# Each pair of last-transform results in a buffer of its own, in a tile whose data are dead

## The chip, the cores and the metric

The kernel runs on one core of one Trainium2 chip. The metric is the device time of one execution, in microseconds (us). Time before: 134.21 us, the median of three runs (134.1 to 134.49).

## The reference

```python
def _A_ref(x, w_r, w_i):                                   # x: 1 x 2048 x 512
    X = jnp.fft.rfft2(x.astype(jnp.float32), axes=(-2, -1))
    X = X * (w_r + 1j * w_i)
    return jnp.fft.irfft2(X, s=(S, D), axes=(-2, -1)).astype(jnp.bfloat16)

def _B_ref(x, w1, b1, w2, b2):
    u = _gelu(jnp.einsum("bsd,sf->bdf", _layernorm(x), w1) + b1)   # S=2048 -> F=1792
    return (jnp.einsum("bdf,fs->bds", u, w2) + b2).transpose(0, 2, 1)

g = _sigmoid((x * gate_w).sum(-1, keepdims=True))
return g * _A_ref(x, w_r, w_i) + (1 - g) * _B_ref(x, w1, b1, w2, b2)
```

All inputs and the output are bfloat16. Branch A filters the 2048 x 512 input in the Fourier domain. Branch B is a layer norm and a two-layer MLP that mixes tokens. A gate g, one number per row, blends the two.

## The kernel before, in words

**Tiling.** The 2048 output rows are cut into 16 blocks of 128, numbered j. Branch B's second product needs, for each j, 14 matmuls of 128x128 by 128x512 (`m2`, L978 to L983) that add up in one PSUM bank. PSUM, the memory in which TensorE leaves its results, has eight banks here: four called `acc`, two `fa`, two `fb`. Block 15 is computed in three column parts (256, 128 and 128 columns), the last two in an `fa` and an `fb` bank.

**The last transform.** Branch A ends with a product with the table `tg` for each j (`i3`, L937 to L946): ten small matmuls for the two blocks of a pair (j, j + 1), five of them into an `fa` bank and five into an `fb` bank. There are eight pairs; I number them 0 to 7. Then:

- `i3ev` (L950 to L955) runs on ScalarE (ACT): it reads one bank, multiplies it by g and writes a half of the pair's tile `eo` ("eviction" below). This frees the bank.
- `es` (L958 to L969) runs on VectorE (DVE): one small copy and two additions or subtractions from `eo` into `es`, two more from `es` back into `eo`, in place. This unfolds a symmetry of the transform. For the last pair (j of at least `LATE` = 14) it first adds a bias (L963), and its results go straight into the output tile `tb_` (shown as `x` in the profile, whose place in memory it takes).
- `yev` (L987 to L990) on ACT moves block j of branch B out of its `acc` bank, with bias and 1 - g, into `tb_`, for j under 14; I call it y with the number of the block.
- `fin` (L992 to L995) on DVE adds a pair's `eo` to `tb_`. For blocks 14 and 15 `fin` is another operation (L998 to L1002), which adds a PSUM bank times 1 - g to `tb_`: one of 512 columns for block 14, then one of 256 and two of 128 for block 15.
- `store` (L1005 to L1009) is a DMA that SyncE (SP) issues: blocks 0-3, 4-7, 8-11, 12-13, 14, and the three parts of 15.

**Buffers.** `eo` has two buffers (`NEO` = 2), 2 KB per partition each. Pair k + 2 can be evicted only when pair k's `fin` has read its buffer. For the last pair, `es` itself is the last reader.

**Order.** Every piece of work is a task with an engine, an estimated duration, its dependencies, a priority, and the buffers that it takes (`alloc`) and gives back (`free`). `Plan.order` (L173 to L239) plays the tasks through an event simulation: whenever an engine is free it takes the ready task with the lowest priority number whose buffers are there. The resulting order is written out, and each engine executes its own list strictly in that order. `i3` has priority 4 and `m2` 20 + j, so a pair's transform goes ahead of the second product as soon as the plan sees an `fa` and an `fb` bank free. On ACT y has priority 1 and an eviction 1.5.

**The tile `B`.** `t["B"]` (L317), 16 KB per partition, holds the spectrum. Its last readers are the matmuls of the transform before this one (`i1`, L856 to L876). After them nobody uses it.

The functions that the diff touches:

Of the kernel before, what the change touches and what calls it, by code (L numbers as in the profile page):

```python
# [13 lines left out]
BF16 = mybir.dt.bfloat16  # L14
F32 = mybir.dt.float32

P = 128
S = 2048
D = 512
NJ = 16  # L20
F = 1792
NFT = 14
L = 256
# [116 lines left out]
class Plan:  # L140
# [11 lines left out]
    def add(self, eng, dur, emit, reads=(), writes=(), prio=0.0, alloc=(), free=(), nbytes=0, after=()):  # L152
        t = Task()
        t.eng, t.dur, t.emit, t.prio = eng, dur, emit, prio
        t.alloc, t.free, t.nbytes = tuple(alloc), tuple(free), nbytes
        t.users, t.end, t.ready = [], None, 0.0
        deps = set(after)
        for k in reads:
            if k in self.last_w:
                deps.add(self.last_w[k])  # L160
            self.readers.setdefault(k, []).append(t)
        for k in writes:
            if k in self.last_w:
                deps.add(self.last_w[k])
            deps.update(self.readers.get(k, ()))
            self.last_w[k] = t
            self.readers[k] = []
        deps.discard(t)
        t.deps = deps
        self.tasks.append(t)  # L170
        return t
# [70 lines left out]
def tt(n):  # L242
    return 0.07 + n / 1920.0
# [10 lines left out]
def act(n, ptr=0):  # L254
    return 0.065 + 0.09 * ptr + n / 1200.0
# [12 lines left out]
def kernel(  # L268
# [22 lines left out]

    pool = ctx.enter_context(tc.tile_pool(name="sb", bufs=1))
    psum = ctx.enter_context(tc.tile_pool(name="ps", bufs=1, space=bass.MemoryType.PSUM))
    NEO, NES = 2, 1

    def sb(shape, dt, tag, bufs=1):
        return pool.tile(shape, dt, tag=tag, name=tag, bufs=bufs)
# [2 lines left out]
        return psum.tile(shape, dt, tag=tag, name=tag, bufs=bufs)  # L300

    NB = {"acc": 4, "fa": 2, "fb": 2}
    caps = {"wa": 1, "wb": 2, "xf": 2, "eo": NEO, "es": NES, **NB}
    pl = Plan(caps)
    add = pl.add
    t = {}
# [156 lines left out]
    for r in range(4):  # L463
# [3 lines left out]
        for b, qs in enumerate(groups):  # L467
            js = [4 * q + r for q in qs]
            xb = [xk[q] for q in qs]
            g = (r, b)  # L470
# [38 lines left out]
            for j in js:  # L509
                if j in HACT:  # L510
                    add("ACT", 0.71, lambda j=j: A.activation(t["h"][:, j // 4, j % 4, :], t["x"][:, j // 4, j % 4, :], ActF.Identity,  # L511
                                                                  bias=t["nmr"][:, j:j + 1], scale=t["rstd"][:, j:j + 1]),
                        reads=xb + [("rstd", *g)] + mvk, writes=[("h", j)], prio=-0.5 + 0.1 * r)
# [19 lines left out]
        for dq in range(4):  # L533
            def fa(r=r, dq=dq):
# [8 lines left out]
                free=["xf"] if dq == 3 else ())  # L543
            add("ACT", act(512), lambda r=r, dq=dq: A.copy(t["X"][:, :, r, :, dq, :], t["pa", r, dq][:]),  # L544
                reads=[("pa", r, dq)], writes=[("X", r, dq)], prio=0, free=["fa"])
# [160 lines left out]
    gates = []  # L706
# [225 lines left out]
    for grp in groups:  # L932
        for j in grp:
            q, r = j // 4, j % 4
            tag = ("fa", "fb")[j % 2]

            def i3(j0=j):  # L937
                g = t["tg"]
                for j in (j0, j0 + 1):
                    p3 = t["i3", j] = ps([P, 2, L], F32, ("fa", "fb")[j % 2], 2)  # L940
                    zv = [xph(h).rearrange("p (q v r a) -> p q v r a", q=4, v=2, r=4)[:, j // 4, :, j % 4, :] for h in range(2)]
                    T.matmul(p3[:, 0, 0:129], lhsT=zv[0][:, 0], rhs=g[:, 0:129], start=True, stop=False)
                    T.matmul(p3[:, 0, 0:129], lhsT=zv[0][:, 1], rhs=g[:, 512:641], start=False, stop=True)
                    T.matmul(p3[:, 0, 129:256], lhsT=zv[0][:, 1], rhs=g[:, 129:256], start=True, stop=True)
                    T.matmul(p3[:, 1, 0:128], lhsT=zv[1][:, 0], rhs=g[:, 256:384], start=True, stop=True)
                    T.matmul(p3[:, 1, 128:256], lhsT=zv[1][:, 1], rhs=g[:, 384:512], start=True, stop=True)  # L946
            if j % 2 == 0:
                add("PE", mm(*[129] * 10), i3, reads=[("z", 0), ("z", 1), "tg"], writes=[("i3", j), ("i3", j + 1)], prio=4, alloc=["fa", "fb"])
                for i in (j, j + 1):
                    def i3ev(j=i):  # L950
                        if j % 2 == 0:
                            t["eo", j // 2] = sb([P, 2, 2, L], BF16, "eo", NEO)
                        A.activation(t["eo", j // 2][:, j % 2], t["i3", j][:], ActF.Copy, scale=t["g"][:, j:j + 1])  # L953
                    add("ACT", act(512, 1), i3ev, reads=[("i3", i), "g"] + ([("eo", j)] if i % 2 else []), writes=[("eo", i)], prio=1.5,
                        alloc=["eo"] if i % 2 == 0 else (), free=[("fa", "fb")[i % 2]])  # L955
                eok = [("eo", j), ("eo", j + 1)]

                def es(j=j + 1):  # L958
                    e, s = t["eo", j // 2], sb([P, 2, 2, 2, P], BF16, "es", NES)
                    o = e if j < LATE else (tbuf(j), t["tb_"][:, j - 1:j + 1])[1]  # L960
                    if j >= LATE:
                        for i in range(2):
                            V.tensor_scalar_add(e[:, i, 0, 0:129], e[:, i, 0, 0:129], t["ombb2"][:, j - 1 + i:j + i])  # L963
                    o = o[:].rearrange("p j h (k d) -> p j (h k) d", k=2)
                    V.tensor_copy(s[:, :, :, :, 0], e[:, :, :, 0:129:128].rearrange("p j h k -> p j k h"))  # L965
                    V.tensor_add(s[:, :, 0, :, 1:P], e[:, :, :, 1:P], e[:, :, :, P + 1:L])
                    V.tensor_sub(s[:, :, 1, :, P - 1:0:-1], e[:, :, :, 1:P], e[:, :, :, P + 1:L])  # L967
                    V.tensor_add(o[:, :, 0:4:3], s[:, :, :, 0], s[:, :, :, 1])  # L968
                    V.tensor_sub(o[:, :, 2:0:-1], s[:, :, :, 0], s[:, :, :, 1])  # L969
                late = j >= LATE  # L970
                add("DVE", tiny(1) + 4 * tt(512) + (0.3 if late else 0), es, reads=(eok + ["omg"]) if late else [],
                    writes=[("o", j), ("o", j + 1)] if late else eok, prio=4, alloc=["es"],
                    free=["eo", "es"] if late else ["es"], after=gates if late else ())

            parts = [slice(0, D)] if j < NJ - 1 else [slice(0, L), slice(L, L + P), slice(L + P, D)]
            for n, cs in enumerate(parts):
                for ft in range(NFT):
                    def m2(ft=ft, j=j, q=q, r=r, n=n, cs=cs):  # L978
                        if ft == 0:
                            t["y", j, n] = ps([P, D], F32, ("acc", "fa", "fb")[n], (4, 2, 2)[n])  # L980
                        w, o = w2at(ft)
                        T.matmul(t["y", j, n][:, cs], lhsT=w[:, o, 512 * q + r:512 * q + 512:4], rhs=t["gl"][:, ft, cs],  # L982
                                 start=(ft == 0), stop=(ft == NFT - 1))  # L983
                    add("PE", mm(cs.stop - cs.start), m2, reads=[("w2", ft), ("gl", ft)], writes=[("y", j, n)], prio=20 + j + 0.3 * n,
                        alloc=[("acc", "fa", "fb")[n]] if ft == 0 else (), after=m1t[-16:-15] if ft == 0 else ())
            if j < LATE:
                def yev(j=j):  # L987
                    A.activation(tbuf(j).rearrange("p h d -> p (h d)"), t["y", j, 0][:], ActF.Identity, bias=t["ombb2"][:, j:j + 1],  # L988
                                 scale=t["omg"][:, j:j + 1])
                add("ACT", act(512, 2), yev, reads=[("y", j, 0), "omg"], writes=[("o", j)], prio=1, free=["acc"], after=gates)  # L990
                if j % 2:
                    def fin(j=j):  # L992
                        o = t["tb_"][:, j - 1:j + 1]
                        V.tensor_add(o, o, t["eo", j // 2][:])  # L994
                    add("DVE", tt(1024), fin, reads=eok, writes=[("o", j - 1), ("o", j)], prio=4, free=["eo"])  # L995
            else:
                for n, cs in enumerate(parts):
                    def fin(j=j, n=n, cs=cs):  # L998
                        o = tbuf(j).rearrange("p h d -> p (h d)")[:, cs]
                        V.scalar_tensor_tensor(o, t["y", j, n][:, cs], t["omg"][:, j:j + 1], o, op0=Alu.mult, op1=Alu.add)  # L1000
                    add("DVE", d1(cs.stop - cs.start) + 0.1, fin, reads=[("y", j, n), "omg", ("o", j)], writes=[("of", j, n)], prio=1,
                        free=[("acc", "fa", "fb")[n]])  # L1002

        for n, cs in enumerate(parts):
            def store(grp=grp, cs=cs):  # L1005
                q, r0, r1 = grp[0] // 4, grp[0] % 4, grp[-1] % 4 + 1
                dma(o4[:, q, r0:r1, cs], t["tb_"][:, grp[0]:grp[-1] + 1].rearrange("p j h d -> p j (h d)")[:, :, cs])
            add("SP", 0.5, store, reads=[("o", j) for j in grp] + [("of", j, n) for j in grp if j >= LATE], prio=50,
                nbytes=256 * (cs.stop - cs.start) * len(grp))  # L1009
# [35 lines left out]
```

## Time and profile before

| | |
|---|---|
| median of the runs | 134.21 us |
| the profiled execution | 134.02 us |
| its span, first to last instruction | 132.2 us |
| PE busy | 124.5 us, 94% |
| DVE busy | 110.8 us, 84% |
| ACT busy | 83.5 us, 63% |
| granted TensorE clock, mean | 0.997 |

How to read it: PE is TensorE's matmuls and PEld its weight loads, DVE is VectorE, ACT is ScalarE, SPq the queue of SyncE, which issues DMAs. A row of the timeline gives its start and its length in us, then the engine, the line of the kernel, the operation, the tile written and the tile read, and how many instructions the row merges. A bracket at the end is the idle time of the engine before the row, and what ended it. Consecutive matmuls overlap, so a row's length is longer than the distance to the next start. Everything that the change touches lies in the last 28 us of the span.

### The profile page before, as it was taken

The page shows a single profiled execution, that of the slowest core. Times are in us where ns is not written, and L with a number is a line of the kernel's source. Part 1 is how long each engine was busy: PE and PEld are TensorE (multiplying, and loading weights), DVE is VectorE, ACT ScalarE, POOL GpSimd, SP SyncE. Part 2 cuts the span into 40 slices and gives each one's busy share as a digit, 9 for nine tenths or more (in the row PEclk, how much of TensorE's full clock was granted, in tenths as well). Part 3 has the DMA queues.
Part 4 walks back from the last instruction along what each step waited for, and adds up shares of the span by engine and source line. Part 5 has one row for each costly group of instructions (what it writes and reads, how often), then busy time and mean ns, then how long its engine had stood idle before and what let it go on. Part 6 is the DMA issues. An engine that isn't in the chain of part 4 may idle for free.

```text
span 132.2 us, 2156 instructions
## 1 busy us (share of the span) xinstructions
PE 124.5 (94%) x766; PEld 70.8 (54%) x780; DVE 110.8 (84%) x248; ACT 83.5 (63%) x166; POOL 0.2 (0%) x4
## 2 busy tenths in 40 slices
PE   6899999999999999999999999999899999999970
PEld 2345454545554575744445555455686665655660
DVE  2689999999999995089999999999859567979790
ACT  4568989599999999993220062322899366583700
POOL 0000000000000000000000000000000000000000
PEclk9999999999999999999999999999999999999998
DMA  3999999936599376999979200000000000330322
GB/s 91 377 359 392 395 394 380 370 79 132 89 272 273 76 159 228 294 397 409 423 299 358 112 0 0 7 0 2 0 0 0 5 0 16 142 159 5 159 79 79
DMA packets 17478, 23.18 MB, mean 175 GB/s; under 512 B 1574, under 2 KB 14908, under 8 KB 17468
## 3 DMA queue, kind: packets, MB, share of 16 engines
q1 hardware_dynamic: 17180, 22.59, 50.3%
q10 hardware_dynamic: 288, 0.46, 1.2%
q8 instruction: 6, 0.10, 0.3%
q14 instruction: 4, 0.03, 0.1%
HBM read 20.93 MB, written 2.10 MB: 174 GB/s over the span
## 4 chain that ended last, share of the span: by engine, by line
DVE 35%; DMA 30%; SPq 13%; PE 11%; issue 4%; ACT 3%; DVEq 0%; ACTq 0%
DMA wa<-in_B_w_dram 15%; SPq L309 13%; PE acc L982 6%; DMA wb<-in_B_w_dram 5%; DMA wt<-in_A_w_i_dram 5%; DMA W<-in_A_w_r_dram 3%; DVE xp L807 3%; DVE st L807 3%; ACT eo L953 3%; DVE xp L812 2%; DVE st L578 2%; DVE B L819 2%; DVE xp L813 2%; DVE eo L968 2%; DVE es L967 2%
## 5 line engine op out<-in xcount | busy, mean ns | idle before, releaser
L982 PE MATMUL acc<-gl,wb 128*128 128x512 bf16 (+1 forms) x108 | 27.2, 372 | 0.3
L982 PE MATMUL acc<-gl,wa 128*128 128x512 bf16 (+1 forms) x109 | 26.4, 372 | 0.1
L684 PE MATMUL acc<-h,wb 128*128 128x512 bf16 x108 | 24.9, 379 | 0.1
L988 ACT ACTIVATE x<-acc,ombb,omg 128x512 bf16<-128x512 f32 x14 | 10.7, 779 | 21.2 <-PE acc L982 21.2
L982 PEld LDWEIGHTS <-wb 128*128 128x128 bf16 x126 | 13.5, 114 | 9.7 <-issue 0.2
L982 PEld LDWEIGHTS <-wa 128*128 128x128 bf16 x126 | 13.5, 114 | 9.6
L684 PE MATMUL acc<-h,wa 128*128 128x512 bf16 x61 | 16.9, 379 | 1.1 <-DVE h L505 0.8
L684 PEld LDWEIGHTS <-wb 128*128 128x128 bf16 x112 | 10.9, 98 | 11.7
L684 PEld LDWEIGHTS <-wa 128*128 128x128 bf16 x112 | 10.3, 98 | 10.8 <-issue 1.9
L700 ACT ACTIVATE gl<-acc,b1f 128x512 bf16<-128x512 f32 x11 | 7.6, 695 | 6.8 <-PE acc L684 6.8
L478 DVE BATCH_NORM_STATS2 stats<-x 128x6 f32<-128x512 bf16 x14 | 9.4, 673 | 2.2 <-DMA x<-in_A_x_dram 2.2
L544 ACT CAST X<-fa 128x512 bf16<-128x512 f32 x16 | 9.3, 583 | 2.6 <-PE fa L541 2.4
L714 ACT ACTIVATE x<-x 128x512 bf16<-128x512 bf16 x16 | 10.1, 657 | 0.0
L511 ACT ACTIVATE h<-x,nmr,rstd 128x512 bf16<-128x512 bf16 x13 | 9.8, 806 | 0.4 <-DVE nmr L502 0.2
L684 PE MATMUL fb<-h,wa 128*128 128x512 bf16 x32 | 9.4, 379 | 0.0
L953 ACT ACTIVATE eo<-fa,g 128x512 bf16<-128x512 f32 x8 | 5.5, 688 | 3.5 <-DVE x L994 3.5
L965 DVE COPY es<-eo 128x8 bf16<-128x8 bf16 x8 | 1.5, 188 | 5.2 <-ACT eo L953 4.8
L684 PE MATMUL fa<-h,wa 128*128 128x512 bf16 x16 | 5.6, 379 | 0.0
L953 ACT ACTIVATE eo<-fb,g 128x512 bf16<-128x512 f32 x8 | 5.5, 691 | 0.0
L359 PE MATMUL fa<-xp 128*128 128x512 bf16 x10 | 4.3, 618 | 1.2 <-DVE xp L320 1.2
L653 ACT CAST B<-fb 128x512 bf16<-128x512 f32 x8 | 5.0, 627 | 0.0
L653 ACT CAST B<-fa 128x512 bf16<-128x512 f32 x8 | 4.9, 615 | 0.0
(177 smaller groups left out, 233.1 us busy)
## 6 DMA issues: line engine op xcount, KB each, us to landing
wb<-in_B_w_dram SPq DMA_DIRECT2D x11, 512.0 KB
wa<-in_B_w_dram SPq DMA_DIRECT2D x7, 512.0 KB
wa<-in_B_w_dram SPq DMA_DIRECT2D x3, 896.0 KB
x<-in_A_x_dram SPq DMA_DIRECT2D x3, 512.0 KB
wb<-in_B_w_dram SPq DMA_DIRECT2D x4, 384.0 KB
out_dram<-x SPq DMA_DIRECT2D x3, 512.0 KB
rot<-dft_ti SPq DMA_DIRECT2D x1, 736.5 KB
rot<-dft_ta SPq DMA_DIRECT2D x4, 160.0 KB
```

The lines of the kernel that those rows point to most:

```text
L309: (eng or nc.sync).dma_start(out=out_ap, in_=in_ap)
L478: V.bn_stats(out=t["stats"][:, j, :], in_=t["x"][:, j // 4, j % 4, :])
L511: add("ACT", 0.71, lambda j=j: A.activation(t["h"][:, j // 4, j % 4, :], t["x"][:, j // 4, j % 4, :], ActF.Identity, bias=t["nmr"][:, j:j ...
L544: add("ACT", act(512), lambda r=r, dq=dq: A.copy(t["X"][:, :, r, :, dq, :], t["pa", r, dq][:]), reads=[("pa", r, dq)], writes=[("X", r, dq ...
L653: A.copy(t["B"][:, lt, e, 2 * c:2 * c + 2, :].rearrange("p s (i b) -> p s i b", b=4), t["pb", lt, e, c][:].rearrange("p s b i -> p s i b"))
L684: T.matmul(t["u", ft][:], lhsT=w[:, j // 4, j % 4, c * P:(c + 1) * P], rhs=t["h"][:, j // 4, j % 4, :], start=(j == jorder[0]), stop=(j == ...
L700: gelus.append(add("ACT", act(512, 1) , lambda ft=ft: A.activation(t["gl"][:, ft, :], t["u", ft][:], ActF.Gelu_apprx_tanh, bias=t["b1f"][: ...
L714: A.activation(t["x"][:, q, r, :], t["x"][:, q, r, :], ActF.Copy, accum_out=t["glog"][:, 4 * q + r:4 * q + r + 1])
L807: V.tensor_mul(o, xs, w)
L953: A.activation(t["eo", j // 2][:, j % 2], t["i3", j][:], ActF.Copy, scale=t["g"][:, j:j + 1])
L982: T.matmul(t["y", j, n][:, cs], lhsT=w[:, o, 512 * q + r:512 * q + 512:4], rhs=t["gl"][:, ft, cs], start=(ft == 0), stop=(ft == NFT - 1))
L988: A.activation(tbuf(j).rearrange("p h d -> p (h d)"), t["y", j, 0][:], ActF.Identity, bias=t["ombb2"][:, j:j + 1], scale=t["omg"][:, j:j + 1])
```

## The change

The tile tag `eo` with its two buffers goes. At pair 0 one tile of eight pairs, 16 KB per partition, is allocated under the tag `B`, that is, in the place of the spectrum; each pair gets its own eighth. The tasks no longer take or give back `eo`, so nothing in the plan bounds how many evicted pairs may be under way except the `fa` and `fb` banks.

```diff
-    NEO, NES = 2, 1
+    NES = 1
...
-    caps = {"wa": 1, "wb": 2, "xf": 2, "eo": NEO, "es": NES, **NB}
+    caps = {"wa": 1, "wb": 2, "xf": 2, "es": NES, **NB}
...
                         if j % 2 == 0:
-                            t["eo", j // 2] = sb([P, 2, 2, L], BF16, "eo", NEO)
+                            if j == 0:
+                                t["eo"] = sb([P, NJ // 2, 2, 2, L], BF16, "B")
+                            t["eo", j // 2] = t["eo"][:, j // 2]
...
-                    add("ACT", act(512, 1), i3ev, ..., writes=[("eo", i)], prio=1.5,
-                        alloc=["eo"] if i % 2 == 0 else (), free=[("fa", "fb")[i % 2]])
+                    add("ACT", act(512, 1), i3ev, ..., writes=[("eo", i)], prio=1.5, free=[("fa", "fb")[i % 2]])
...
-                    free=["eo", "es"] if late else ["es"], after=gates if late else ())
+                    free=["es"], after=gates if late else ())
...
-                    add("DVE", tt(1024), fin, reads=eok, ..., prio=4, free=["eo"])
+                    add("DVE", tt(1024), fin, reads=eok, ..., prio=4)
```

No instruction is added or removed. Since the plan is made from these tasks, the engines' lists change, as they stand in the kernel as built:

- **ACT.** Before: y8, y9, four evictions, y10, four evictions, y11, four, y12, two, y13, two. After: y8, y9, ten evictions, y10, six evictions, y11, y12, y13. Of the waits before an eviction, those on DVE for a buffer are gone, except that the very first eviction waits for what DVE and one DMA did with the spectrum; all other evictions wait for PE alone, or for nothing.
- **PE.** The list is the same up to its entry 1276 and from 1425 on, of 1562. Between, pairs 4 to 7 come earlier among the second product's matmuls: pair 4 three matmuls after pair 3, then pair 5 after three more, pair 6 after three, pair 7 after six. Before, pair 4 came 17 matmuls after pair 3, and pair 7 followed the second matmul of block 13.
- **DVE.** The same list but for one step: the addition of pair 6 (`fin`) goes behind `es` of pair 7.
- **SP.** The same stores in the same order.

More of the change, by code (lines that the diff above doesn't have):

```diff
@@ L951, in i3ev @@
                         if j % 2 == 0:
-                            t["eo", j // 2] = sb([P, 2, 2, L], BF16, "eo", NEO)
+                            if j == 0:
+                                t["eo"] = sb([P, NJ // 2, 2, 2, L], BF16, "B")
+                            t["eo", j // 2] = t["eo"][:, j // 2]
                         A.activation(t["eo", j // 2][:, j % 2], t["i3", j][:], ActF.Copy, scale=t["g"][:, j:j + 1])
-                    add("ACT", act(512, 1), i3ev, reads=[("i3", i), "g"] + ([("eo", j)] if i % 2 else []), writes=[("eo", i)], prio=1.5,
-                        alloc=["eo"] if i % 2 == 0 else (), free=[("fa", "fb")[i % 2]])
+                    add("ACT", act(512, 1), i3ev, reads=[("i3", i), "g"] + ([("eo", j)] if i % 2 else []), writes=[("eo", i)], prio=1.5, free=[("fa", "fb")[i % 2]])
                 eok = [("eo", j), ("eo", j + 1)]
@@ L994, in fin @@
                         V.tensor_add(o, o, t["eo", j // 2][:])
-                    add("DVE", tt(1024), fin, reads=eok, writes=[("o", j - 1), ("o", j)], prio=4, free=["eo"])
+                    add("DVE", tt(1024), fin, reads=eok, writes=[("o", j - 1), ("o", j)], prio=4)
             else:
```

## Prediction

> **What bounds the kernel now.** I read the table of waits first, because the change takes a wait away, then the timeline of the last 28 us, where all of it happens. From the table of waits (who waited for whom: us in total, times, longest):
>
> ```profile
> ACT x L988 <- PE acc L982: 21.2, 8, 7.7
> ...
> DVE es L965 <- ACT eo L953: 4.8, 4, 2.4
> ACT eo L953 <- DVE x L994: 3.5, 2, 2.3
> ```
>
> The last two make a ring: the eviction waits for the buffer that `fin` (L994) gives back, and `es` waits for the eviction. ACT's wait for PE is harmless: there is work enough on PE. The timeline shows one turn of the ring:
>
> ```profile
> 120.88 1.28 DVE L994 TENSOR_TENSOR x<-x,eo 128x1024 bf16<-128x1024 bf16 x2
> ...
> 121.66 0.69 ACT L953 ACTIVATE eo<-fa,g 128x512 bf16<-128x512 f32 x1 [2.27 <-DVE x L994]
> ...
> 122.25 0.68 ACT L953 ACTIVATE eo<-fb,g 128x512 bf16<-128x512 f32 x1
> ...
> 122.96 0.19 DVE L965 COPY es<-eo 128x8 bf16<-128x8 bf16 x1 [0.79 <-ACT eo L953]
> ```
>
> ACT sat idle for 2.27 us until `fin` released the buffer, and then DVE idled for 0.79 us until both halves were there. The same bracket of 0.79 stands at 112.22 and at 117.59: three turns, 2.37 us of DVE idle. PE pays too, once:
>
> ```profile
> 117.03 0.22 PE L942 MATMUL fa<-tg,xp 128*128 128x129 bf16 x1
> 117.03 0.10 PEld L943 LDWEIGHTS <-xp 128*128 128x128 bf16 x1 [0.23 <-issue]
> ```
>
> Pair 5's transform needs a bank that the eviction at 116.29 (0.69 us) empties only at 116.98; for the second half 0.26 us are lost in the same way. Now the end:
>
> ```profile
> 127.41 0.55 PE L982 MATMUL fb<-gl,wb 128*128 128x128 bf16 x7
> 127.52 1.14 DVE L1000 SCALAR_TENSOR_TENSOR x<-acc,omg,x 128x512 bf16<-128x512 f32 x2
> 128.57 0.34 DVE L1000 SCALAR_TENSOR_TENSOR x<-fa,omg,x 128x128 bf16<-128x128 f32 x1
> 128.83 0.34 DVE L1000 SCALAR_TENSOR_TENSOR x<-fb,omg,x 128x128 bf16<-128x128 f32 x1
> ```
>
> PE's last result is there at 127.96, but DVE only then gets to blocks 14 and 15: `es` of the last pair held it to 127.4. It finishes at 129.17. And because four pieces become ready in a bunch, SP is late as well:
>
> ```profile
> 128.29 1.77 SPq L309 DMA_DIRECT2D out_dram<-x  x4
> ```
>
> Four stores in 1.77 us, each 0.35 long: about 0.47 from start to start, so the last is issued at 129.71, 0.54 after its data. From there to the end of the span (132.24) it is 2.53 us. So the end is set by DVE, delayed by the ring, then SP; PE was ready 1.2 us before DVE.
>
> **The change, part by part.** No instruction is added or removed; all durations are from this execution.
>
> *ACT.* The waits for buffers go. Evictions back to back start 0.575 us apart (110.93, 111.51, 112.08, 112.65). The first still starts at 105.57, as now: the row before it on ACT, y9, sets that. Its new wait, for the spectrum's users, costs nothing: the DMA into `B` was issued at 89.75, and DVE last wrote `B` at 94.72. Ten evictions end at 105.57 + 10 x 0.575 = 111.32; y10 needs block 10's matmuls, done by 111.24 (below), and takes 0.67 (104.90 to 105.57). The next eviction starts at 111.99, and the sixteenth at 114.87. y11 to y13 follow as PE delivers, and none is needed before DVE's `fin`.
>
> *PE.* A 128x512 matmul takes 0.216 from start to start (seven between 109.96 and 111.47), one of the transform 0.056, a pair 0.56. The lists part at 108.45. Left there: 40 transform matmuls, 2.23; 63 of 128x512 (seven of block 10, all of 11 to 14), 13.59; block 15, 14 x (0.109 + 0.056 + 0.056) = 3.08. Together 18.90, so PE issues its last at 127.35, if it never stalls. Today it does so at 127.80 (127.41 + 7 x 0.056): the difference, 0.45, is the stall at 117. Does the new order stall elsewhere? Each half of a pair needs the bank that the same half of two pairs earlier left. The tightest is pair 4's second half: PE reaches it at 108.45 + 0.65 + 0.28 = 109.38, and its bank is emptied by the sixth eviction, 105.57 + 5 x 0.575 + 0.69 = 109.14. The later ones have 0.3 (pair 5: 110.58 against 110.29; pair 6: 111.79 against 111.44; pair 7: 113.64 against 113.26). So no stall, but little room: I take nothing for it, and as the other end 0.7 (below). The last result lands 0.16 after its issue (0.55 - 0.39), at 127.51.
>
> *DVE.* `es` of one pair takes 1.74 up to the next `es` (112.22 to 113.96), 1.55 up to a `fin` (113.96 to 115.51), and two `fin` take 2 x 0.61. Four steps make 4.51. It starts at 106.86 as now, and with data always there it goes 111.37, 115.88, 120.39; pair 6's `es` to 121.94, the bias 0.45, pair 7's `es` 1.69 (125.76 to 127.45): 124.08; the moved `fin` 0.69: 124.8. Evictions and y are all done earlier (y13 by 122.3). So block 14 can be added at 124.8 instead of 127.52, 2.7 us sooner; PE has it by 124.5. If DVE alone decided, the end would be 129.17 - 2.7 = 126.5. It doesn't: PE is late next. The last part of block 15 starts 0.05 after PE's last result (y9 starts at 104.90, after matmuls that end at 104.85), at 127.56, takes 0.34, and its store is issued 0.03 later (a `fin` ends at 125.39 and its store starts at 125.42): 127.93.
>
> *SP.* Pieces are now ready at about 124.8, 125.5, 126.4, 127.2 and 127.9; at 0.47 each they don't bunch, so the 0.54 go. I keep 2.53 from the last issue to the end; less company for the last transfer could take a little off, and the earlier 512 KB stores are long over.
>
> *Sum.* 129.71 - 127.93 = 1.78 us: 0.45 PE's stall, 0.79 DVE's lag behind PE, 0.54 SP's bunch. Against the profiled execution's 134.02 that is 132.24; it lies 0.19 under the median of the runs, so for a median I forecast 134.21 - 1.78, about **132.4**. Bounds: no tail at all gained from SP would make the gain 1.24, a transfer tail 0.3 shorter (part of the 0.47 at which neighbours follow) makes it 2.1. The forecast's own range is 132.0 to 133.0.
>
> **The rivals.**
>
> *Evictions slow down PE.* ACT now evicts 16 times almost without a pause, at 1.15 a pair, where PE needs 0.56 + 3 x 0.216 = 1.21 between pairs. If an eviction in this burst cost 0.67, as y does, pair 7's second half would wait for an eviction that starts at 105.57 + 12 x 0.67 = 113.61 and ends at 114.30, plus 0.05: 0.71 after PE gets there. The gain shrinks to 1.07: 133.1. Against it: the eight rows of back-to-back evictions stand at 0.57 to 0.58.
>
> *Only PE's own loss comes back.* If DVE still ends 1.2 behind PE and SP still bunches, the gain is PE's 0.45: 133.8. That asks for 2.7 us of new DVE time, and nothing is added to DVE; its idle brackets say the opposite. In the Trainium skill, "Perfetto Trace Analysis", section "Identifying the Most-Contended Engine", the engine with the highest occupancy is the one to work on; by it PE, at 94%, would be the limit, and a change that takes no work from PE would return no more than PE's stall, 0.45. The trace agrees for the time up to 127.96 and not behind it.
>
> *One tile, one wait (the slower side).* All pairs now lie in one tile. If each eviction waited until DVE's in-place writes of the pair before were done, as it would with a dependency on the whole tile, then a pair would cost 0.575 + 0.69 + 0.03 for the evictions and 1.63 for `es`: 2.9, eight in a row from 105.57, 128.9; then one `fin` and blocks 14 and 15 (0.69 + 0.75 + 0.39 + 0.26 + 0.34): 131.3 instead of 129.17, 2.1 later: about 136.1. It decides from about 2.65 a pair. Against it: in the kernel as built, no eviction but the first waits for DVE. What else could slow DVE on this place, a worse layout, speaks in the rows too: operations of 128x1024 into `B` (L583, 0.60 from start to start) take what `fin` takes (0.61).
>
> *It does nothing* (the tail is bound by something that the profile doesn't show): 134.2.
>
> **How the numbers follow.** Forecast 0.74, slowed evictions 0.10, only PE's loss 0.06, nothing 0.03, slower 0.07. The forecast's case and the slowed evictions hold 0.84; allowing for misses at their edges the range is 132.0 to 133.2. A measurement here tells about 0.3%, 0.4 us, from no change: faster by more than that 0.88 (0.74 + 0.10 + two thirds of the third case), within it 0.05, slower 0.07.
>
> **What would show it.** Right: no bracket "<-DVE x L994" before an eviction; evictions ten in a row from 105.6; no 0.79 before `es`; no stall of PE before a transform; DVE idle ahead of the last three L1000, each released by PE; PE's last matmul near 127.5; stores not bunched; last store near 127.9. Wrong: PE brackets at the transforms of pairs 4 to 7 (slowed evictions), DVE ending over 0.5 us after PE (the second rival), evictions waiting for DVE (the third), or a longer way from the last store to the end than 2.5 us.

## The result, and the profile after

The changed kernel takes **132.38 us** (median of four runs, 132.32 to 132.53), the kernel before 134.27 (median of four, 134.1 to 134.49). The ratio is 0.986, with a 95% interval of 0.9843 to 0.9877: 1.4% faster. The prediction was 132.4. In the profiled execution the span fell from 132.24 to 130.46, by 1.78; its device time fell by less, from 134.02 to 132.39. Outside the span lie 1.78 us before and 1.93 us after, and no row of the profile says why.

The table of waits of the changed kernel, the rows that belong to the last stage (us in total, times, longest):

```profile
ACT x L989 <- PE acc L983: 22.7, 8, 7.9
...
DVE es L966 <- ACT B L955: 2.4, 1, 2.4
...
DVE x L1001 <- PE acc L983: 0.8, 1, 0.8
...
DVE x L1001 <- PE fb L983: 0.4, 1, 0.4
...
DVE x L1001 <- PE fa L983: 0.3, 1, 0.3
```

The row of evictions that wait for DVE is gone. `es` waits for ACT once, at the very start of the stage, where four waits stood before. And the additions of block 15 now wait for PE, three times: DVE gets there first.

The timeline of the changed kernel at the end of the run of evictions:

```profile
110.13 0.75 ACT L955 ACTIVATE B<-fa,g 128x512 bf16<-128x512 f32 x1
...
110.70 0.76 ACT L955 ACTIVATE B<-fb,g 128x512 bf16<-128x512 f32 x1
...
111.29 0.83 ACT L989 ACTIVATE x<-acc,ombb,omg 128x512 bf16<-128x512 f32 x1
...
111.97 0.73 ACT L955 ACTIVATE B<-fa,g 128x512 bf16<-128x512 f32 x1
```

The ninth and tenth eviction start at 110.13 and 110.70, y10 at 111.29 without a bracket, the next eviction at 111.97. I had put y10 at 111.32 and the eviction at 111.99. The end of the timeline:

```profile
127.00 0.55 PE L983 MATMUL fb<-gl,wb 128*128 128x128 bf16 x7
127.59 0.35 DVE L1001 SCALAR_TENSOR_TENSOR x<-fb,omg,x 128x128 bf16<-128x128 f32 x1 [0.43 <-PE fb L983]
```

```profile
127.97 0.33 SPq L309 DMA_DIRECT2D out_dram<-x  x1
```

DVE waits 0.43 for PE's last result, adds it, and SP stores it 0.03 later, alone. The chain of work that ended last says the same. Over the whole span PE's share of it went from 11% to 58% and DVE's from 35% to 28%, but for this change the last stage counts. In the kernel before, the chain leaves PE behind block 10's matmuls, goes through y10 to the evictions of pair 2, and from there back and forth between DVE and ACT:

```profile
108.88 1.26 PE acc L982 x5
...
110.17 0.71 ACT x L988
...
110.93 0.55 ACT eo L953
```

In the changed kernel it stays on PE from the start of the stage up to DVE's last addition:

```profile
116.91 9.08 PE acc L983 x49
```

**How I compare executions from here on.** Both kernels and all experiments have the same instructions up to the first eviction, but it starts anywhere from 105.57 to 107.60 in these profiled executions; two of the late ones are 2 us late. What lies before the stage thus adds a scatter that the change has no part in, and it is in the medians too. So besides the medians I give the stage, from one execution each: from the start of the first eviction to the end of the span, and on the way to the end of DVE's last addition and to the start of the last store. The last store's start is read from its own row, since the rows of a bunch differ in length. In the kernel before, the four are 0.33, 0.42, 0.40 and 0.38 long, and the last is

```profile
129.68 0.38 SPq L309 DMA_DIRECT2D out_dram<-x  x1
```

The prediction took each as 0.35 long and so put the last one at 129.71.

| kernel | first eviction at | to DVE's end | to the last store | to the end of the span | median, us |
|---|---|---|---|---|---|
| before | 105.57 | 23.60 | 24.11 | 26.67 | 134.27 |
| changed | 105.58 | 22.36 | 22.39 | 24.88 | 132.38 |
| e1, eight buffers, old order | 106.17 | 22.37 | 22.40 | 24.91 | 132.85 |
| e2, before, two queues for stores | 107.56 | 23.59 | 23.63 | 26.17 | 133.82 |
| e3, before, last pair copied | 105.82 | 22.78 | 22.88 | 25.43 | 133.28 |
| e4, three buffers | 105.66 | 22.88 | 22.91 | 25.41 | 133.47 |
| e5, changed, 0.87 us more PE | 105.58 | 23.24 | 23.27 | 25.77 | 133.49 |
| e6, changed, three more DVE additions | 105.64 | 22.37 | 22.55 | 25.09 | 132.89 |
| e7, changed, eight more DVE additions | 106.44 | 24.29 | 24.82 | 27.38 | 135.66 |
| e8, changed, slower evictions | 106.05 | 23.03 | 23.06 | 25.57 | 133.24 |
| e9, two buffers in the dead tile | 107.60 | 23.64 | 24.15 | 26.70 | 134.56 |
| e10, four buffers in the dead tile | 106.20 | 22.68 | 22.71 | 25.21 | 133.01 |

The changed kernel's stage is 1.79 us shorter. The last store is 2.49 to 2.51 us ahead of the end where it was issued alone, and 2.54 to 2.56 where stores came in a bunch or, in e2, on two queues. The medians of e1 to e10 were taken beside the kernel before at 134.23 (e1 to e4), 134.24 (e5 to e8) and 134.58 (e9, e10). The medians of e1, e4, e6 and e10 lie 0.4 to 0.6 above what I expected, while their stages lie within 0.2 of it. I go by the stage there. No experiment says what the rest of those medians is.

### The profile page after: what moved, and what is told of

Same layout as the page of the kernel before. It is cut to its first block, busy times and chain, and to the rows that moved or that the text cites. A ratio compares the mean times of both kernels' runs of the same rounds, so it can differ in the third digit from the quotient of the medians.

```text
span 130.5 us, 2166 instructions
## 1 busy us (share of the span) xinstructions
PE 125.4 (96%) x780; PEld 70.7 (54%) x780; DVE 110.6 (85%) x248; ACT 83.1 (64%) x166; POOL 0.2 (0%) x4
## 4 chain that ended last, share of the span: by engine, by line
PE 58%; DVE 28%; DMA 8%; issue 2%; ACT 2%; SPq 0%; DVEq 0%
PE acc L684 18%; PE acc L983 17%; DMA wa<-in_B_w_dram 5%; PE fb L684 5%; DVE xp L807 3%; DVE st L807 3%; DMA x<-in_A_x_dram 2%; PE fa L684 2%; PE fa L538 2%; DVE xp L812 2%; DVE st L578 2%; DVE B L819 2%; DVE xp L813 2%; PE fb L868 1%; PE fa L868 1%
## 5 line engine op out<-in xcount | busy, mean ns | idle before, releaser
L983 PE MATMUL acc<-gl,wa 128*128 128x512 bf16 (+1 forms) x112 | 27.2, 372 | 0.0
L684 PE MATMUL acc<-h,wb 128*128 128x512 bf16 x112 | 25.9, 379 | 0.0
L684 PE MATMUL acc<-h,wa 128*128 128x512 bf16 x64 | 17.8, 387 | 0.6 <-DVE h L505 0.6
L955 ACT ACTIVATE B<-fb,g 128x512 bf16<-128x512 f32 x8 | 5.9, 735 | 0.0
L955 ACT ACTIVATE B<-fa,g 128x512 bf16<-128x512 f32 x8 | 5.8, 727 | 0.0
L709 DVE TENSOR_TENSOR x<-x,gw 128x2048 bf16<-128x2048 bf16 x4 | 4.8, 1216 | 0.0
```

The costliest lines, as they stand in the source:

```text
L684: T.matmul(t["u", ft][:], lhsT=w[:, j // 4, j % 4, c * P:(c + 1) * P], rhs=t["h"][:, j // 4, j % 4, :], start=(j == jorder[0]), stop=(j == ...
L709: add("DVE", tt(2048), lambda r=r: V.tensor_mul(t["x"][:, :, r, :], t["x"][:, :, r, :], t["gw"][:, None, :].to_broadcast([P, 4, D])), read ...
```

## The experiments

My theory: the two buffers tie ACT and DVE into a ring; without it the end moves from DVE and SP to PE, and the gain has three terms, PE's stall (0.45), DVE's lag behind PE (0.79) and the bunch of stores on SP (0.54). The main rival at this point: the new order of the lists does it, not the buffers. Others: the stores' bunch is worth nothing, the place in memory matters, and PE is not what sets the new end.

### e1: eight buffers, the old order

```diff
-                            t["eo", j // 2] = sb([P, 2, 2, L], BF16, "eo", NEO)
+                            if j == 0:
+                                t["eo"] = sb([P, NJ // 2, 2, 2, L], BF16, "B")
+                            t["eo", j // 2] = t["eo"][:, j // 2]
```

in the kernel before, with the plan's count of two left as it was.

> Eight buffers in the dead tile, but the plan still counts two, so every engine's list stands in the order of the kernel before. If the buffers are what counts (my account): the evictions of pairs 4 to 7 no longer wait for DVE, though some now wait behind y on ACT; PE has no stall at pair 6, issues its last matmul at 127.35 as in the changed kernel, DVE adds block 14 by about 126.1, and the last store goes at 127.9 to 128.0: 132.3 to 132.5 us, like the changed kernel. If the new order of the lists is what counts (transforms pulled forward on PE, ten evictions in a row on ACT), nothing is gained: 134.2 us.

Measured: 132.85 us, ratio to the kernel before 0.989 (0.9839 to 0.9941); the stage takes 24.91, against 24.88 in the changed kernel. Its end in the timeline:

```profile
112.73 0.18 DVE L967 COPY es<-B 128x8 bf16<-128x8 bf16 x1 [0.64 <-ACT B L955]
...
127.41 0.35 DVE L1002 SCALAR_TENSOR_TENSOR x<-fa,omg,x 128x128 bf16<-128x128 f32 x1
...
128.19 0.35 DVE L1002 SCALAR_TENSOR_TENSOR x<-fb,omg,x 128x128 bf16<-128x128 f32 x1 [0.43 <-PE fb L984]
```

The last addition waits 0.43 for PE, the same as in the changed kernel, while the one before it has no wait. DVE starts to add block 14 at 126.24, that is 20.07 after the first eviction, against 18.96 in the changed kernel and 21.95 in the one before: it arrives later than in the changed kernel, and it makes no difference at the end. The median is 0.4 above what I expected, and the first eviction of this execution is 0.6 later than in the changed kernel; ahead of the stage its weight loads wait 2.2 us in total for `wb`, against 1.2. So the new order is worth nothing that the stage shows; the buffers are worth all of it.

The first line above corrects the prediction. Of its three waits of 0.79 before `es`, the first stands here too, at 0.64, without any ring: in the old order y10 lies ahead of pair 2's evictions on ACT and waits for PE. So that wait belonged to the order for the most part, and the ring made the other two.

### e2: the bunch of stores alone

In the kernel before, the store of block 14 and that of the second part of block 15 are issued by ACT:

```diff
+            sq = "ACT" if (grp[0] == 15 and n == 1) or grp[0] == 14 else "SP"
...
-            add("SP", 0.5, store, ...
+            add(sq, 0.5, store, ...
```

> The kernel before, with the stores of block 14 and of block 15's second part issued by ACT, the others by SP as they were. My account has 0.54 us of the kernel before in the bunch of four stores on one queue, 0.47 apart: with two queues the last store goes within 0.05 of its data at 129.2 instead of 129.71, so about 0.5 us less, 133.7. If the bunch costs nothing (the transfers or the end of the program decide), no change: 134.2.

Measured: 133.82 us, ratio 0.9976 (0.9942 to 1.0011), which by itself doesn't tell 0.4 us from nothing. The stage tells it. The two queues in its timeline:

```profile
130.81 0.34 DVE L1000 SCALAR_TENSOR_TENSOR x<-fb,omg,x 128x128 bf16<-128x128 f32 x1
```

```profile
130.28 1.00 ACTq L309 DMA_DIRECT2D out_dram<-x  x2
...
130.67 0.85 SPq L309 DMA_DIRECT2D out_dram<-x  x2
```

DVE ends at 131.15, as late after the first eviction as in the kernel before (23.59 against 23.60), but the last store starts at 130.67 + 0.85 - 0.33 = 131.19, 0.04 after its data instead of 0.51. The stage is 0.50 shorter, near the 0.54 of the term.

### e3: DVE's part alone

In the kernel before, the last pair is copied instead of unfolded:

```diff
+                    if j >= LATE:
+                        V.tensor_copy(o, e[:])
+                        return
                     o = o[:].rearrange("p j h (k d) -> p j (h k) d", k=2)
```

> The kernel before, but for the last pair the unfolding is left out: a plain copy of the evicted pair into the output tile stands in its place (the output of blocks 14 and 15 is not the transform's). That takes 1.1 to 1.4 us from DVE ahead of the last additions and leaves the ring of two buffers and PE's stall as they are. My account: DVE's lag behind PE (0.79) goes and most of the bunch of stores (0.54) with it, PE's 0.45 stay: 132.9 to 133.1. If PE were the end of the kernel before, no change: 134.2. If DVE alone decided, all of the 1.1 to 1.4 plus the bunch would come off: 132.4.

Measured: 133.28 us, ratio 0.9914 (0.9881 to 0.9947). The stage is 1.24 shorter than before, where the two terms together are 1.33; the last store still trails its data by 0.1. The ring and PE's stall are there unchanged, and yet the last addition now waits for PE:

```profile
117.28 0.10 PEld L943 LDWEIGHTS <-xp 128*128 128x128 bf16 x1 [0.23 <-issue]
...
121.90 0.69 ACT L953 ACTIVATE eo<-fa,g 128x512 bf16<-128x512 f32 x1 [2.27 <-DVE x L997]
...
128.25 0.35 DVE L1003 SCALAR_TENSOR_TENSOR x<-fb,omg,x 128x128 bf16<-128x128 f32 x1 [0.31 <-PE fb L985]
```

So relieving DVE alone gives most of the gain, and what remains to the changed kernel (25.43 against 24.88) is PE's stall and the rest of the bunch. This also kills the rival that only PE's own loss comes back.

### e4, e10 and e9: how many buffers, and where

e4 is the kernel before with `NEO` = 3, which is all that the memory holds beside the rest.

> The kernel before with three buffers of their own instead of two, which is all that the memory holds. My account, with the durations of the trace put through the lists of this kernel: DVE never idles between pairs, as with eight, but the evictions of pairs 3, 5 and 6 still wait for a buffer, and PE stalls by 0.1 to 0.25 at three transforms, so PE ends about 0.5 later than with eight, near where it did with two; DVE's lag and the bunch go: 132.7 to 132.9 us. If it takes all eight buffers, 133.5 or more; if three are as good as eight, 132.3 to 132.4.

Measured: 133.47 us, ratio 0.9947 (0.9902 to 0.9993); the stage 25.41, 1.26 shorter than before. I expected a gain of 1.3 to 1.5, so a little less came; by the medians it is 0.76. The evictions of pairs 3 and 5 wait still:

```profile
111.03 0.69 ACT L953 ACTIVATE eo<-fa,g 128x512 bf16<-128x512 f32 x1 [1.80 <-DVE x L994]
...
115.51 0.69 ACT L953 ACTIVATE eo<-fa,g 128x512 bf16<-128x512 f32 x1 [1.40 <-DVE x L994]
```

but DVE doesn't, and PE ends 127.60 - 105.66 = 21.94 after the first eviction (start of its last row), against 21.84 in the kernel before and 21.42 in the changed one. DVE's lag and the bunch are gone, PE's stalls have moved to the transforms of pairs 5, 6 and 7: there the second half starts 0.22 to 0.24 after the last matmul of the first half, instead of 0.06. The last addition waits 0.43 for PE here too.

e10 has four buffers, in the dead tile, and the plan counts four:

```diff
-    NEO, NES = 2, 1
+    NEO, NES = 4, 1
...
-                            t["eo", j // 2] = sb([P, 2, 2, L], BF16, "eo", NEO)
+                            if j == 0:
+                                t["eo"] = sb([P, NEO, 2, 2, L], BF16, "B")
+                            t["eo", j // 2] = t["eo"][:, j // 2 % NEO]
```

> Four buffers in the dead spectrum tile, the plan counting four. My account, with measured durations put through this kernel's lists: DVE never idles between pairs; one eviction (pair 6's second half) comes late enough to hold PE by about 0.2 us; 25.0 to 25.1 us from the first eviction to the end of the span, against 24.88 with eight and 25.41 with three: 132.5 us. If all eight are needed: 25.4 or more, like three.

Measured: 133.01 us, ratio 0.9883 (0.9841 to 0.9925); the stage 25.21, between three buffers and eight, 0.1 more than I expected. Two evictions wait for DVE, pair 4's by 0.71 and pair 6's by 1.39, and PE idles for 0.26 at one transform, the second half of pair 6:

```profile
111.64 0.69 ACT L955 ACTIVATE B<-fa,g 128x512 bf16<-128x512 f32 x1 [0.71 <-DVE x L996]
...
112.96 0.10 PEld L943 LDWEIGHTS <-xp 128*128 128x128 bf16 x1 [0.26 <-issue]
...
116.12 0.69 ACT L955 ACTIVATE B<-fa,g 128x512 bf16<-128x512 f32 x1 [1.39 <-DVE x L996]
```

No stall of PE follows the second wait.

e9 is e10 with `NEO` = 2: the place alone.

> The kernel before, with its two buffers laid into the dead spectrum tile and nothing else changed: the place alone. My account: the place costs and gains nothing, the ring waits as before: 134.2 us, and 26.6 to 26.7 us from the first eviction to the end of the span. If the place matters (one tile with waits of its own, or slower access), it is slower, or faster, by that.

Measured: 134.56 us beside 134.58, ratio 1.0002 (0.9958 to 1.0047); the stage 26.70, against 26.67. Its table of waits has the ring as before:

```profile
DVE es L967 <- ACT B L955: 4.8, 4, 2.4
ACT B L955 <- DVE x L996: 3.5, 2, 2.3
```

The place costs nothing and gains nothing. It only makes room.

### e5: does PE set the new end?

```diff
                         w, o = w2at(ft)
+                        for _ in range(8 if (j, n, ft) == (15, 0, 0) else 0):
+                            T.matmul(t["y", j, n][:, cs], lhsT=..., rhs=..., start=True, stop=True)
```

> The changed kernel with eight extra 128x256 matmuls ahead of block 15's first part, whose result the next matmul overwrites: 8 x 0.109 = 0.87 us of PE and nothing else. If PE sets the end of the changed kernel (my account), all of it shows: about 133.2 to 133.3 us, and 0.87 more from the first eviction to the end of the span (24.88 us in the changed kernel, 26.67 in the one before). If DVE or the stores set it, little or nothing shows: 132.4.

Measured: 133.49 us. The stage is 0.89 longer than the changed kernel's, for 0.87 of added PE work: all of it shows. DVE only waits longer for PE, 1.61 instead of 0.75:

```profile
126.91 0.48 DVE L1003 SCALAR_TENSOR_TENSOR x<-acc,omg,x 128x256 bf16<-128x256 f32 x1 [1.61 <-PE acc L985]
```

### e6 and e7: how much room does DVE have now?

```diff
                     V.tensor_sub(o[:, :, 2:0:-1], s[:, :, :, 0], s[:, :, :, 1])
+                    for _ in range(3 if j >= LATE else 0):          # 8 in e7
+                        V.tensor_add(s[:, 0], s[:, 0], s[:, 1])
```

> The changed kernel with three extra additions of 128x512 (0.35 us each from start to start) on DVE behind the last pair's unfolding: 1.05 us. My account: DVE idled for 0.75 + 0.30 + 0.43 ahead of the last three additions of the changed kernel, so the extra work is hidden: 132.4 us, at most 0.1 more from the first eviction to the end. If DVE still sets the end: 1.05 more, 133.4.

Measured: 132.89 us. DVE ends 22.37 after the first eviction, as without the extra work (22.36): it is hidden, though it took 1.26 (124.13 to 125.39) and not 1.05. The stage is nonetheless 0.21 longer, because the stores bunch: the last one starts 0.18 after its data instead of 0.03, and its way to the end is 0.05 longer.

```profile
127.66 0.35 DVE L1003 SCALAR_TENSOR_TENSOR x<-fb,omg,x 128x128 bf16<-128x128 f32 x1 [0.27 <-PE fb L985]
```

```profile
128.19 0.38 SPq L309 DMA_DIRECT2D out_dram<-x  x1
```

The data are there at 128.01, the store starts at 128.19, behind one that was issued at 127.69. I had overlooked that the room on SP is smaller than the room on DVE.

> The same with eight extra additions, 2.8 us, which is more than DVE's 1.48 of idle time. My account: the additions of blocks 14 and 15 start at about 127.35 and follow one another without a wait, the last ends at about 129.1 instead of 127.94, and the stores bunch on SP again, 0.47 apart, so the last is issued at about 129.5 instead of 127.97: 1.5 to 1.6 more from the first eviction to the end, 133.9 us. If the bunch costs nothing, only DVE's 1.15 shows: 133.5. If DVE's room were smaller than its idle time, up to 2.8: 135.2.

Measured: 135.66 us, the stage 2.50 longer, where I expected 1.5 to 1.6. The eight additions took more than I put in:

```profile
124.92 3.64 DVE L972 TENSOR_TENSOR es<-es 128x512 bf16<-128x512 bf16 x8
```

Eight in 3.64 us, the next operation 3.56 after the first: 0.445 each instead of 0.35. Each reads what the one before it wrote, and the rows of `es` show the same two distances: in the kernel before, L967 starts 0.34 after L966, on which it does not depend, and L968, which reads what L967 wrote, starts 0.45 after L967 (106.94, 107.28, 107.73). Of these 3.56, DVE's end moved by 1.93, so 1.63 were hidden (I had counted 1.48 of idle time); the bunch of stores adds 0.51 again, and the way to the end 0.06. 1.93 + 0.51 + 0.06 = 2.50. The mechanism stands; my duration for this operation was wrong.

### e8: how little room do the evictions have?

```diff
                         A.activation(t["eo", j // 2][:, j % 2], t["i3", j][:], ActF.Copy, scale=t["g"][:, j:j + 1])
+                        A.copy(t["mv"][:, j, 0:1], t["g"][:, j:j + 1])
```

> The changed kernel with one tiny ACT operation (a column of g copied into a column of the statistics, dead by then) behind each eviction, about 0.2 us, so that an eviction takes 0.75 to 0.8 from start to start instead of 0.57. My account of the little room (0.25 to 0.4 us at each transform, all measured with evictions at 0.57): PE now stalls at each of the pairs 3 to 7, by 0.3 to 0.4 per pair, 1.6 to 2.1 in all, and the gain of the change is about gone: 133.9 to 134.4 us. If ACT has room enough off the path, no change: 132.4.

Measured: 133.24 us, the stage 0.69 longer than the changed kernel's, where I expected 1.6 to 2.1. The added operation was cheaper than I thought:

```profile
106.05 0.68 ACT L955 ACTIVATE B<-fa,g 128x512 bf16<-128x512 f32 x1
106.62 0.19 ACT L956 COPY mv<-g 128x1 f32<-128x1 f32 x1
106.70 0.70 ACT L955 ACTIVATE B<-fb,g 128x512 bf16<-128x512 f32 x1
```

It is 0.19 long, but the next eviction starts 0.08 after it: 0.65 from eviction to eviction, later 0.66. PE stalls where I said, at each of the pairs 3 to 7, but only in the second half and by 0.13 to 0.15 per pair instead of 0.3 to 0.4. Pair 3, where the distance is 0.18 instead of 0.06:

```profile
108.60 0.22 PE L946 MATMUL fa<-tg,xp 128*128 128x128 bf16 x1
...
108.78 0.22 PE L942 MATMUL fb<-tg,xp 128*128 128x129 bf16 x1
```

For evictions at 0.67 the prediction's rival had worked out 0.71 of stall, all of it at pair 7. With 0.66, 0.69 came, spread over five transforms. So the room of 0.25 to 0.4 us at each transform is real and is used up soon.

## Why the prediction was right, point by point

- **The ring goes.** Right: no eviction waits for DVE, and the 0.79 us before `es` are gone three times over. But only two of the three were the ring's. The first was for the most part y10's (0.64 of it stays in e1), and it went because the new order evicts pair 2 before y10.
- **PE's stall, 0.45.** PE is through with issuing its last matmul at 127.00 + 7 x 0.056 = 127.39 instead of 127.80, so 0.41; the prediction had 127.35. One label in the working was wrong: the transform that stalls at 117.03 belongs to pair 6, not to pair 5. It waits for pair 4's eviction, the one at 116.29, so the sum isn't touched.
- **DVE's lag behind PE, 0.79.** DVE ended 1.21 after PE's last result (129.17 against 127.96); now 0.39 (127.94 against 127.55): 0.82. (The prediction's split gives 0.03 too little here and 0.03 too much to the bunch: the issue of a store trails its data by 0.03 even alone.) Block 14's addition starts at 124.54, for which I had 124.8.
- **The bunch of stores, 0.54.** The last store trailed its data by 0.51, not 0.54 (it started at 129.68), and now does by 0.03: 0.48. e2 got 0.50 from this term alone, 0.02 of it on the way to the end.
- **The way from the last store to the end**, which I kept at 2.53, was 2.56 before and measured 2.49: 0.07. The sum of the four, 0.41 + 0.82 + 0.48 + 0.07 = 1.78, is the difference of the spans, and the 1.78 of the prediction. The mechanism and the order of size of each term were right; that the sums agree to the last digit is luck, since the misses of the terms (up to 0.07) cancel.
- **The median, 132.4 against 132.38.** Here too some luck: the forecast took the span's 1.78 off the earlier median of 134.21. The spans did differ by 1.78, but the medians by 1.89 and the device times of the profiled executions by 1.63.
- **PE is late next.** Shown by e5 (0.89 for 0.87), and by e6, where DVE's additions don't move the last addition.
- **Slowed evictions** didn't come about: an eviction stays at 0.57 from start to start. Evictions slowed to 0.66 cost 0.69 (e8), near the 0.71 that the rival gave for 0.67.
- **Only PE's own loss comes back.** Refuted: PE's own loss was 0.41, and e3 takes nothing from PE and gets 1.24. PE was the busiest engine of the span and not the last one at its end. One figure in this rival needs a correction: PE's 94% is the share of the span in which some matmul was under way. The section of the Trainium skill that the rival names, "Identifying the Most-Contended Engine" in "Perfetto Trace Analysis", says that for TensorE this share is not a good measure of how close a kernel is to roofline, and asks for MFU (the matmuls' FLOPs over the peak) and for the busy share of the weight loads instead. The rows of this case leave PE the busiest engine by its work, too: the changed kernel's trace has 780 matmuls with 284,730 columns, and at 0.216 us per 512 columns that is an estimated 91% of the span before, against DVE's 84%. That didn't make it the engine that ended last.
- **One tile, one wait.** No such wait in the trace, and e9 shows that the place is neutral.
- What I hadn't seen: that the reordering which comes with the change is worth nothing at the end (e1), because PE, and not DVE, is then late.

## What to carry to other kernels

A ring of buffers between two engines is seen by its pair of rows in the table of waits, each engine waiting for the other; price it by what ends the stage, not by the waits (here DVE idled for 2.4 us ahead of `es`, about 0.6 of it not the ring's doing, and the stage gained 1.8), and ask who is late next. A tile whose data are dead is room that cost nothing here (e9), and it needn't hold everything: of the 1.79 us, three buffers gave 1.26, four 1.46. Pieces that become ready in a bunch pay for the queue that issues their stores, so an engine that is late at the end is charged twice.

## What the runs showed of the hardware that I had not expected

- In the run of evictions each row gets longer, from 0.68 to 0.77 us, and y10 0.83 instead of 0.78, while the distance from start to start stays at 0.57. So the length of an ACT row says less of its cost than the distance to the next one. Why the rows grow is open; no run was made for it.
- A tiny ACT operation behind an eviction is 0.19 us long but delays the next one by 0.08 (e8); DVE additions that depend on each other take 0.445 us from start to start, where the rows of `es` that don't depend on each other take 0.34 to 0.35 (e7, e6).
- After a bunch the last store's own row is 0.38 us long instead of 0.33, and its way to the end of the span 2.54 to 2.56 instead of 2.49 to 2.51.
- The part ahead of this stage, the same in all kernels, ended up to 2 us apart from one execution to another (first eviction at 105.57 to 107.60). In part it can be read from the waits for loads: in e9 DVE's first statistics wait 3.0 us for the input, where they wait 2.2 in the changed kernel, and in e1 PE's weight loads wait 2.2 us in total for `wb` around 70 to 75 us, where they wait 1.2. What makes the loads late wasn't tried.
